# An adaLN linear-attention and MLP block on one core: w_mod's products on TensorE directly, and the first two k projections side by side

## The chip, the core and the metric

The kernel runs on 1 core of a Trainium2 chip. The core has TensorE (matrix products, PE in the profile; PEld is its loading of weights), VectorE (DVE), ScalarE (ACT), GpSimd (POOL) and SyncE (SP), which issues DMAs. The metric is device time in microseconds (us). Times are the median of several executions; a profile is one execution recorded by the hardware profiler.

## What is computed

The inputs are x (2048 tokens, D = 576 features), wqkv (576 x 1728), wo (576 x 576), w1 (576 x 4608), w2 (4608 x 576), a condition c (1 x 576) and w_mod (576 x 3456), all in float32. Cut to what matters, the reference is:

```
mod = silu(c) @ w_mod                     # six vectors of 576: sa, ca, ga, sb, cb, gb
h = layernorm(x) * (1 + ca) + sa
q, k, v = split(h @ wqkv)                 # 32 heads of 18 features
kv = sum over tokens of phi(k) x v;  z = sum over tokens of phi(k)
x = x + ga * ((phi(q) kv / (phi(q) z)) @ wo)
h = layernorm(x) * (1 + cb) + sb
x = x + gb * (silu(h @ w1) @ w2)
```

with phi(t) = t + 1 for positive t and exp(t) otherwise, plus 1e-6. sa and ca are needed before the first projection. They are the first third of w_mod ("piece 0", 1152 columns: 576 for the shift, 576 for the scale).

## The kernel before, in words

Tokens are worked in 16 tiles of 128, in four blocks of four tiles. The 576 features are cut in five chunks along the contraction, four of 128 and a tail of 64. Operands of the large products are split in a high and a low part (float32r), so a projection of one tile is a row of 14 passes over chunk and part (`x_passes`, L208), each pass with two products of about half the output columns: 28 products a tile.

**The opening (L255 to L375)** is written in a fixed order on all engines (`manual_schedule`). SP issues the loads: c, the four x tiles of block 0, piece 0 of w_mod in five chunks, then wqkv in three groups (k, v, q) of five chunks; the tail's rows are loaded twice, into partitions 0 to 63 and 64 to 127. The silu of c stands as a column per chunk in `sc`. The product c @ w_mod is made in two ways:

- the first chunk of w_mod goes to TensorE directly (`mod_mm`, L272): stationary is a 128-column piece of w_mod, moving a 128 x 128 tile that holds the chunk's c in every column (`scb`);
- the other four chunks are multiplied by their c and summed on VectorE (L334 to L339) into `sums`, which TensorE then turns into columns with a tile of ones (`mod_cols`, L347).

The result is one column of shift and one of scale per chunk (`cols["a"]`, L352). Meanwhile the four x tiles are normalised (`LayerNorm`, L151) and transposed on TensorE (L331) into PSUM banks, one of 512 columns per chunk: the four tiles side by side. Each chunk is then modulated over all 512 columns (L185 on ScalarE, L187 on VectorE) and split in high and low part (`split_h`, L189: a copy on ScalarE L191, a subtraction on VectorE L109) into `hT`. Chunks go in the order 0, 2, 4, 1, 3. The weights' high parts are copies on ScalarE (`w_hi`, L281), their low parts subtractions on VectorE or GpSimd (`w_lo`, L284).

**The loop over the 16 tiles (L478)** does per tile the k projection (`k_proj`, L423) with phi, the v projection (`v_proj`, L431), the product of keys and values of the tile before (`kv_mm`, L446), and on some tiles a q projection (`q_proj`, L441). PSUM has two large buffers for projections (`ps2`, name psK), one bank for transposes (`psT`) and the sums of keys and values (kvp). The block after is normalised and transposed (`turn`, L470) inside the loop. The other two thirds of w_mod are summed on VectorE at tiles 5 and 8 (`mod_piece`, L378) from three raw buffers. In the loop a planner orders each engine's instructions by its own estimate of time; `behind(...)` holds work back until given instructions have been issued.

**After the loop** (from L528) come the last q projections, the attention output, and the MLP in two-block units. Some lists of order are written out by hand (`ORDERS`, L64); they begin after the loop.

## Time and profile before

| | us |
|---|---|
| median of 3 runs | 1156.73 (1156.49 to 1158.33) |
| the profiled execution, whole | 1160.13 |
| its span, first to last instruction | 1158.4 |
| TensorE busy in the span | 1135.1 |
| VectorE busy | 977.3 |
| GpSimd busy | 659.7 |
| ScalarE busy | 527.8 |

A line of a group view reads: source line, engine, operation, output and inputs, shapes, count | busy us in all, mean ns of one | idle time of the engine before it, and what ended that. A line of the timeline reads: start, length, engine, line, operation, count, and in brackets idle time before it and who ended it. Neighbouring instructions of one kind are one line there. A line of waits reads: who waited for whom, us in total, times, longest. Matmuls are pipelined: the length of a single one includes the way through the array, so the cost of many is read from a group's length.

### The profile page before, as it was taken

The numbers are of one execution on the slowest core, as the hardware profiler recorded it, in microseconds if no ns is written. First come the engines' busy times: TensorE is split into PE (matmuls) and PEld (weight loads), VectorE is DVE, ScalarE is ACT, GpSimd is POOL, SyncE is SP. The second block draws the span as 40 slices with busy tenths as digits, with TensorE's granted clock in tenths as the row PEclk, the third lists the DMA queues.
The fourth block names the chain that finished last, engine by engine and source line by source line (L and its number), as shares of the span: only waits on it lengthen the run. The fifth ranks groups of instructions, "written<-read, shape, count | busy, mean of one in ns | idle before, by whom it ended". The sixth has DMA issues, their size and how long they took to land.

```text
span 1158.4 us, 19498 instructions
## 1 busy us (share of the span) xinstructions
PE 1135.1 (98%) x7173; PEld 1049.7 (91%) x7173; DVE 977.3 (84%) x1540; ACT 527.8 (46%) x1074; POOL 659.7 (57%) x749
## 2 busy tenths in 40 slices
PE   4999999999999999999999999999999999999998
PEld 4999999999998889999999999999999999999998
DVE  6747664478797999999999999999999999999996
ACT  4443343336656445444444444454444444444541
POOL 4300000254635495776777677767757766776686
PEclk9999999999999999999999999999999999999999
DMA  9213300123157978869769769778687697697684
GB/s 284 105 42 93 113 6 1 32 69 130 41 230 268 377 260 305 320 251 350 274 253 349 273 252 364 265 278 334 260 329 299 251 352 272 253 354 274 251 311 154
DMA packets 57213, 268.61 MB, mean 232 GB/s; under 512 B 5466, under 2 KB 19294, under 8 KB 34078
## 3 DMA queue, kind: packets, MB, share of 16 engines
q1 hardware_dynamic: 57118, 267.36, 62.8%
q8 instruction: 57, 0.93, 0.3%
q14 instruction: 38, 0.31, 0.1%
HBM read 250.56 MB, written 16.78 MB: 231 GB/s over the span
## 4 chain that ended last, share of the span: by engine, by line
PE 94%; DMA 2%; DVE 1%; ACT 1%; issue 0%; SPq 0%; ACTq 0%; DVEq 0%
PE up L1142 33%; PE down L1215 32%; PE psK L212 13%; PE big L212 7%; PE small L705 2%; PE big L716 2%; PE kvp L452 1%; DMA acc<-in_A_wqkv_dram 1%; PE psK L599 1%; PE big L631 1%; PE small L200 1%; DVE hT L109 1%; PE psT L200 1%; DMA hT<-in_w_mod_dram 1%; PE up L1245 1%; PE down L1245 1%
## 5 line engine op out<-in xcount | busy, mean ns | idle before, releaser
L1223 DVE TENSOR_TENSOR acc<-down,acc 128x576 f32<-128x576 f32 x330 | 246.0, 753 | 13.3 <-PE down L1215 3.3
L1142 PE MATMUL up<-hT,w 128*128 128x512 f32 x916 | 240.3, 391 | 0.0
L1142 PEld LDWEIGHTS up<-hT,w 128*128 128x128 f32 x916 | 164.5, 188 | 25.8
L1177 POOL TENSOR_TENSOR s<-f,f 128x256 f32<-128x256 f32 x66 | 51.7, 784 | 163.8 <-ACT f L1158 163.8
L1215 PE MATMUL down<-w,hb 128*128 128x288 f32 x792 | 120.7, 294 | 0.0
L1215 PE MATMUL down<-w,hc 128*128 128x288 f32 x792 | 120.7, 294 | 0.0
L1215 PEld LDWEIGHTS down<-w,hb 128*128 128x128 f32 x792 | 113.5, 188 | 6.1 <-DVE U L1223 0.5
L1215 PEld LDWEIGHTS down<-w,hc 128*128 128x128 f32 x792 | 113.6, 188 | 5.6
L212 PE MATMUL psK<-w,hT 128*128 128x288 f32 (+1 forms) x704 | 112.7, 300 | 3.1 <-DVE hT L109 2.1
L1223 DVE TENSOR_TENSOR U<-down,U 128x576 f32<-128x576 f32 x132 | 99.5, 753 | 17.4 <-PE down L1215 15.1
L109 DVE TENSOR_TENSOR w<-v,w 128x288 fp32r<-128x288 f32 (+1 forms) x170 | 111.9, 668 | 0.4 <-ACT w L885 0.4
L212 PEld LDWEIGHTS psK<-w,hT 128*128 128x128 f32 x704 | 100.8, 191 | 4.4 <-DVE hT L109 3.1
L1142 PE MATMUL up<-room,w 128*128 128x512 f32 x348 | 93.2, 396 | 0.9 <-DVE f L1163 0.9
L1196 POOL TENSOR_TENSOR hc<-s,hc 128x512 fp32r<-128x512 f32 x66 | 89.7, 1359 | 0.0
L1158 ACT ACTIVATE f<-f 128x512 f32<-128x512 f32 x102 | 64.4, 631 | 47.8 <-DVE f L1163 25.4
L1161 DVE TENSOR_TENSOR f<-up,p 128x512 f32<-128x512 f32 x102 | 69.7, 683 | 15.4 <-PE up L1142 9.7
L1142 PEld LDWEIGHTS up<-room,w 128*128 128x128 f32 x348 | 62.4, 188 | 12.2 <-DVE f L1163 1.4
L885 ACT CAST w<-v 128x288 fp32r<-128x288 f32 x85 | 36.6, 434 | 77.0 <-PE down L1215 54.3
L1181 POOL TENSOR_TENSOR f<-f,s 128x256 f32<-128x256 f32 x66 | 50.9, 772 | 34.4 <-DVE hb L1196 28.7
L1215 PE MATMUL down<-w,hd 128*128 128x288 f32 x396 | 63.2, 295 | 0.0
L1215 PE MATMUL down<-w,he 128*128 128x288 f32 x396 | 63.1, 295 | 0.0
L1215 PE MATMUL down<-w,ha 128*128 128x288 f32 x396 | 63.0, 294 | 0.0
(281 smaller groups left out, 2468.8 us busy)
## 6 DMA issues: line engine op xcount, KB each, us to landing
hT<-hd SPq DMA_DIRECT2D x66, 1280.0 KB, 6.0
hT<-hd SPq DMA_DIRECT2D x45, 1024.0 KB, 5.1
room<-hd SPq DMA_DIRECT2D x35, 1280.0 KB, 5.6
room<-hd SPq DMA_DIRECT2D x20, 1024.0 KB, 5.6
v<-in_B_w_dram SPq DMA_DIRECT2D x17, 576.0 KB
v<-in_B_w_dram SPq DMA_DIRECT2D x17, 512.0 KB, 7.8
hd<-S SPq DMA_DIRECT2D x6, 1024.0 KB, 4.2
xt<-in_A_x_dram SPq DMA_DIRECT2D x16, 288.0 KB, 4.2
```

What stands on the lines that cost most here:

```text
L109: return V.tensor_sub(lo, full, f32(hi))
L200: T.transpose(ps[:, i * P : (i + 1) * P], xt[i][:, cidx * P : (cidx + 1) * P], ident)
L212: T.matmul(ps, xpart(a), wpart(b), start=n == 0, stop=n == len(XW) - 1)
L885: A.copy(self.w2[n][:, 0], src)
L1142: T.matmul(ps, left, right, start=first and m == 0, stop=m == len(seq) - 1, skip_group_check=True)
L1158: A.activation(self.f[i, k], self.f[i, k], AF.Silu)
L1161: V.tensor_add(f, self.bank[bank[1]], self.p1)
L1177: G.tensor_add(self.s[:, 0:1], half(i, 0, 1), half(i, 1, 1))
L1181: G.tensor_sub(half(i, 1, 0), half(i, 1, 0), self.s[:, 1:2])
L1196: eng.tensor_sub(t[:, :, 1, :], src, f32(t[:, :, 0, :]))
L1215: T.matmul(ps[:, p, :HALF], self.a[i, n][:, u, p * P : (p + 1) * P], self.w.w2[n][:, v], start=n in (1, 5, 7, 6) and j == 0, stop=j == 2, ...
L1223: V.tensor_add(dst, ps[:, :, :HALF], dst)
```

## The change

- **Loads.** c is loaded from ScalarE's queue instead of SP's. c's tail is written twice into its row, so that the tail's c stands in partitions 0 to 63 and again in 64 to 127. w_mod's tail of piece 0 is loaded from ScalarE's queue in two loads: the rows' shift half into partitions 0 to 63, their scale half into 64 to 127. Chunks are loaded in order 0 to 4.
- **w_mod.** Chunks 0 and 1 (`mod_direct`) and the tail go to TensorE directly. The moving operand is a single column of c; for the tail it is a tile of two columns, `sel`, so that one product gives shift and scale. VectorE sums chunks 2 and 3 only, first the columns of feature chunks 0 and 1 (HEAD = 2), then the rest (`add_mod`, `col_mod`); TensorE turns these sums with one column of ones.
- **Block 0 in two halves.** Tiles 0 and 1 are transposed, modulated and split first (256 columns a chunk). As each chunk is ready, `k_part` runs its first two passes for both tiles; the passes with the weights' low parts and those of the tail follow, tile by tile. So both k projections fill both large PSUM buffers at the same time. Their phi (`k_phi`) and the split of the result (`k_split`) are written out in the opening too, as are the splits of v's weights.
- **The second half.** Tiles 2 and 3 are transposed, modulated and split (`turn_half`) beside the v projections of tiles 0 and 1. Scratch for the halves is the three raw buffers.
- **The loop.** TensorE's instructions are kept in the order of the program text; k of tiles 0 and 1 is left out. In `x_passes` the chunks go 0 to 4.

The core of the diff:

```diff
-    CHUNKS = (0, 2, 4, 1, 3)
+    CHUNKS, START = (0, 2, 4, 1, 3), range(KC + 1)
     XW = []
-    for k in CHUNKS:
+    for k in START:
...
-    nc.sync.dma_start(crow[0:KC, :], c[0, 0 : KC * P].rearrange("(j p) -> j p", p=P))
-    nc.sync.dma_start(crow[KC : KC + 1, 0:64], c[0:1, KC * P : D])
-    xts = [load_x(0, i) for i in range(4)]
+    nc.scalar.dma_start(crow[0:KC, :], c[0, 0 : KC * P].rearrange("(j p) -> j p", p=P))
+    nc.scalar.dma_start(crow[KC : KC + 1, :].rearrange("p (h r) -> p h r", h=2),
+                        c[0:1, KC * P : D].unsqueeze(1).to_broadcast([1, 2, 64]))
+    xts = x0s = [load_x(0, i) for i in range(4)]
...
+    load_mod(mods[0], 0, 0)
+    for a in range(2):
+        nc.scalar.dma_start(tmod[a * 64 : a * 64 + 64, 0:D], w_mod[KC * P : D, a * D : (a + 1) * D])
+    for k in range(1, KC):
         load_mod(mods[k], 0, k)
...
+    def mod_mm(m, k, rhs, a=None, first=False, last=False):
+        c = 2 * (k - HEAD if k >= HEAD else k)
+        dst = mod_ps_a[k >= HEAD][:, c : c + 2] if a is None else mod_ps_a[k >= HEAD][:, c + a : c + a + 1]
+        T.matmul(dst, m[:, k * P : (k + 1) * P], rhs, start=first, stop=last, skip_group_check=True)
+
+    def mod_direct(m, rhs, first=False):
+        A.copy(m[:, :, D:DX], m[:, :, KC * P : D])
+        for k in START:
+            for a in range(2):
+                mod_mm(m[:, a], k, rhs, a, first and k in (0, HEAD) and a == 0)
+
+    def add_mod(k0, k1):
+        o = sums[:, :, k0 * P : min(k1 * P, D)]
+        V.scalar_tensor_tensor(o, mods[3][:, :, k0 * P : min(k1 * P, D)], sc[:, 3:4], o, op0=ALU.mult, op1=ALU.add)
...
+    def turn_half(chunks):
+        t = psT()
+        pT = {k: t[:, n * 256 : n * 256 + 256] for n, k in enumerate(chunks)}
+        turn_tiles(pT, (2, 3), chunks)
+        for k in chunks:
+            modulate_split(*half_args(1, k, pT))
+
+    def k_part(tiles, passes, first=False, last=False):
+        for n, (a, b) in enumerate(passes):
+            for i in tiles:
+                for h in range(2):
+                    T.matmul(kps[i][:, h, :HALF], hT[0][:, a, i * P : i * P + P], wk_(b)[:, h * HALF : (h + 1) * HALF],
+                             start=first and n == 0, stop=last and n == len(passes) - 1)
...
+        mod_direct(mods[0], sc[:, 0:1], True)
+        A.copy(tmod[:, D:DX], tmod[:, KC * P : D])
+        for k in START:
+            mod_mm(tmod, k, sel)
+        ln.normalise(0, xts[0], xts[0], V)
+        ln.normalise(1, xts[1], xts[1], A)
...
+        turn_tiles(pT, (0, 1), range(KC))
+        mod_direct(mods[1], sc[:, 1:2])
+        for i in (2, 3):
             ln.normalise(i, xts[i], xts[i], A)
...
+        add_mod(0, HEAD)
+        col_mod(0, HEAD)
+        modulate(*args[0], V)
+        w_hi(wk_, 0, acc[0])
+        split_h(*args[0])
+        modulate(*args[1], A)
+        add_mod(HEAD, KC + 1)
+        first_k(0)
+        col_mod(HEAD, KC + 1)
...
+        for k in START:
+            w_lo(wk_, k, acc[k], G if k < 3 else V)
+        for i in range(2):
+            k_part([i], [(k, KC + k) for k in START[:KC]] + [(2 * KC + 1, 2 * KC), (2 * KC, 2 * KC)], last=True)
...
+        a0 = k_phi(kps[0])
...
+        first = *k_split(0, a0), pool
+        after = *k_split(1, k_phi(kps[1])), pool
...
-    for t in range(NT):
+    with tc.manual_schedule(engines={mybir.EngineType.PE}):
+        for t in range(NT):
...
+            if t > 1:
+                k_proj(t)
...
+            if t == 0:
+                with behind(first):
+                    turn_half((0, 1))
             before, after = after, v_proj(t)
+            if t == 0:
+                with behind(first):
+                    for k in START:
+                        split_w(wqp_, k, acc[10 + k], G)
+                    turn_half((2, 3))
+            if t == 1:
+                turn_half((4,))
```

More of the change, by code (lines that the diff above doesn't have):

```diff
@@ L270 @@
     vx = [pa.tile([P, NHC, 2, P], F32R, name=f"vx{i}") for i in range(2)]
-    def mod_mm(ps, m, kp, k, rhs, first, last):
-        for a in range(2):
-            T.matmul(ps[:, a * P : (a + 1) * P], m[:kp, a, k * P : (k + 1) * P], rhs,
-                     start=first and a == 0, stop=last, skip_group_check=True)
     def mod_ps(k):
@@ L295, with k_phi, k_split @@
+    def k_phi(ps):
+        a = pa.tile([P, D], F32, name="a")
+        phi(ps, a, pa)
+        return a
+    def k_split(t, a):
+        return A.copy(pk[t % 2][:, 0, :D], a), sub_hi(pk[t % 2][:, 1, :D], a, pk[t % 2][:, 0, :D])
     wk_, wv_ = cut(wkv, 0, D), cut(wkv, D, D)
-    ND = 1
-    scb = pa.tile([P, D], F32, name="e", bufs=2)[:, : ND * P].rearrange("p (k q) -> p k q", k=ND)
-    sums = mods[ND]
+    sums = mods[2]
+    sel = pa.tile([P, 2], F32, name="sel")
+    h32 = [pa.tile([P, 2, D], F32, name="raw", bufs=3).rearrange("p a d -> p (a d)") for _ in range(3)]
@@ new lines, in col_mod, with turn_tiles @@
+    def col_mod(k0, k1):
+        for k in range(k0, k1):
+            for a in range(2):
+                mod_mm(sums[:, a], k, ones[:, 0:1], a, last=True)
+        V.tensor_add(cols["a"][:, k0:k1, :], mod_ps_a[k0 >= HEAD].rearrange("p (k a) -> p k a", a=2),
+                     plus1.unsqueeze(1).to_broadcast([P, k1 - k0, 2]))
+    def turn_tiles(pT, tiles, chunks):
+        for i in tiles:
+            for k in chunks:
+                T.transpose(pT[k][:, i % 2 * P : i % 2 * P + P], x0s[i][:, k * P : (k + 1) * P], ident)
```

225 lines of the change are left out of this document (101 added, 124 removed).

## The prediction

> **What bounds the kernel now.** I read the page first (shares, then the chain that ended last), then TensorE's stretches, its waits, and the order of its instructions in the first 60 us.
>
> ```profile
> span 1158.4 us, 19498 instructions
> ...
> PE 1135.1 (98%) x7173; PEld 1049.7 (91%) x7173; DVE 977.3 (84%) x1540; ACT 527.8 (46%) x1074; POOL 659.7 (57%) x749
> ...
> PE 94%; DMA 2%; DVE 1%; ACT 1%; issue 0%; SPq 0%; ACTq 0%; DVEq 0%
> ```
>
> TensorE carries 94% of the last chain. The rest is the opening, so the next view cuts TensorE's time there (columns: stretch, length, busy time and instructions, granted clock, DMA share, GB/s).
>
> ```profile
> core 0: us, PE busy (x), PEclk, DMA share, GB/s
> 9.80:13.00 3.20, 3.17 (x15) 1.00 1.04 392
> 13.00:16.40 3.40, 2.97 (x27) 1.00 1.06 245
> 16.40:19.80 3.40, 1.16 (x8) 1.00 1.04 274
> 19.80:23.20 3.40, 3.27 (x14) 0.50 1.06 293
> 23.20:26.60 3.40, 2.05 (x12) 1.00 1.06 338
> 26.60:30.00 3.40, 1.68 (x9) 1.00 1.05 299
> 30.00:33.40 3.40, 3.40 (x15) 0.50 1.06 399
> 33.40:60.00 26.60, 26.60 (x204) 1.00 0.13 50
> 60.00:240.00 180.00, 177.46 (x1307) 1.00 0.16 48
> 240.00:1158.40 918.40, 913.11 (x5572) 1.00 0.73 271
> ```
>
> From 30 us on there is next to no idle time: 2.5 us up to 240, 5.3 us after. So a gain is work that TensorE has finished earlier when it becomes continuously busy, and it lasts to the end. There are holes before 30 us, and two stretches at half clock, each after a thinly used one.
>
> ```profile
> 9.80 3.80 PEld L275 LDWEIGHTS kvp<-e,hT 128*128 128x128 f32 x20 [5.63 <-issue]
> 9.83 3.96 PE L275 MATMUL kvp<-e,hT 128*128 128x128 f32 x20 [5.57 <-DMA hT<-in_w_mod_dram]
> ...
> 15.36 1.42 DVE L339 SCALAR_TENSOR_TENSOR hT<-hT,sc 128x1152 f32<-128x1152 f32 x1 [1.11 <-DMA hT<-in_w_mod_dram]
> ...
> 18.28 1.40 ACT L282 CAST w<-acc 128x576 fp32r<-128x576 f32 x2 [5.28 <-DMA acc<-in_A_wqkv_dram]
> ...
> 22.64 0.75 PE L212 MATMUL psK<-w,hT 128*128 128x288 f32 x2
> ...
> 32.83 2.84 PE L212 MATMUL psK<-w,hT 128*128 128x256 f32 x18
> ...
> 54.00 0.50 PE L212 MATMUL psK<-w,hT 128*128 128x288 f32 x2
> ```
>
> The rows give the opening's dates: the first w_mod chunk lands at 9.8, the last full one at 15.4, k's first weights at 18.3. Tile 0's k projection begins at 22.64, v of tile 0 at 32.8, and k of tile 2 at 54.0. Between 22.6 and 32.8 only one k projection is done, because:
>
> ```profile
> PE psK L212 <- DVE hT L109: 2.1, 4, 0.8
> PE kvp L275 <- DVE hT L339: 2.0, 1, 2.0
> PE psK L212 <- ACT hT L191: 0.9, 1, 0.9
> ```
>
> TensorE waits for VectorE's sum of w_mod (L339) and then, chunk by chunk, for the split of the block (L191, L109).
>
> **The yardstick.** I compare the date at which k of tile 2 begins. By then the kernel before has also done the key-value product of tile 1 (10 instructions) and four transposes, which the new order puts later: 10 x 0.133 (3.73/28, below) and 4 x 0.14 (2.2/16) = 1.9 us. So the date to beat is 54.0 - 1.9 = 52.1.
>
> **The change, priced from these rows.**
>
> ```profile
> 1.26 0.36 SPq L256 DMA_DIRECT2D crow<-in_c_dram  x1
> ...
> 49.95 3.73 PE psK L212 x28
> ...
> 108.03 1.28 PE L396 MATMUL psK<-ones,tmod 128*128 128x128 f32 x10
> ...
> L333 PE MATMUL psK<-ident,xt 128*128 128x128 f32 x16 | 2.2, 272 | 0.0
> ...
> L187 DVE TENSOR_SCALAR a<-psT,col_a 128x512 f32<-128x512 f32 x1 | 0.8, 801 | 0.0
> ...
> L191 ACT CAST hT<-h 128x512 fp32r<-128x512 f32 x2 | 1.2, 620 | 0.0
> ...
> L109 DVE TENSOR_TENSOR hT<-e,hT 128x512 fp32r<-128x512 f32 x2 | 2.6, 1290 | 0.0
> ...
> L414 DVE TENSOR_SCALAR a<-psK 128x576 f32<-128x576 f32 x3 | 2.3, 756 | 2.1 <-ACT e L409 2.1
> ...
> L409 ACT ACTIVATE e<-psK 128x576 f32<-128x576 f32 x5 | 3.2, 646 | 5.3 <-PE psK L212 5.3
> ```
>
> *Loads.* c moves from SP to ScalarE's queue, so the x tiles are issued two issues earlier; w_mod's tail (288 KB) travels beside them. The bytes are the same, and the DMA share is full anyway. I take the first w_mod chunk at 10.0 instead of 9.8, the last full one unchanged at 15.4. The four issues on ScalarE stand ahead of work that isn't needed before 10 us; without that cover they would cost some 1.4 us (4 x 0.36, SP's issue of c).
>
> *w_mod on TensorE.* Two full chunks and the tail are multiplied directly: 10 + 10 + 5 products, each recorded as two instructions, with one or two columns moving instead of 128. VectorE loses two of its four sums (1.4 us for a full chunk) ahead of the first column. The trace has no one-column product. Bounds: zero, and the price with 128 columns, 0.128 us an instruction (1.28/10) or, from a standing start, 0.198 (3.96/20). I take 0.09 and 0.17, near the top, because the weight loads alone fill 3.80 of the 3.96 us and none is saved. Then: 10.0 + 20 x 0.17 = 13.4; the tail, 10 x 0.09, 14.3; eight transposes at 0.14 (2.2/16), 15.4; second chunk, 1.8, 17.2. VectorE's sum for the first two columns (512 of 1152 elements, 0.63 us after 15.4) is ready at 16.0, so TensorE is late, not VectorE. Four more products, 0.7, and the small addition, taken at 0.2: the first columns stand at X = 18.1. With a free one-column product VectorE sets X at 16.2; with 128-column prices X is 20.2.
>
> *First half-block.* Only 256 columns are modulated and split, so modulation (0.80) and split copy (0.62) become about 0.45 and 0.36; the subtraction (1.29 on the mean, 0.65 by size) is taken at 0.5, as GpSimd's subtractions run beside fewer of them. First k products at X + 0.9. VectorE then sums the other three columns (0.79 + 0.2), TensorE turns them (12 x 0.09 = 1.1), and chunk 1 begins at X + 3.9. From there ScalarE is the pace: cast of weights 0.67, split 0.36, part of the modulation, some 1.1 us a chunk, against 8 x 0.133 = 1.07 on TensorE. Chunk 3 ends at X + 7.5. The last two low parts of the weights follow on VectorE (taken at 0.75 each, like L414's pass over 576 columns) and the remaining 24 products end at X + 11.2 = 29.3: both k projections done, where before one was done at 32.8.
>
> *v of tile 0* needs a bank of tile 0's k: exponent and maximum (0.65 + 0.76) end at 29.3 behind four weight splits on VectorE. It begins at 29.4. Then 28 products for each of v0, v1, q0, q1 (4 x 3.73), one key-value product (1.33) and ten transposes of the second half, no longer in an idle stretch (1.4): 29.4 + 17.65 = 47.05. Against 52.1 that is 5.1 us.
>
> *What is late next.* The second half's transposes share one bank, so chunks 2 and 3 wait for ScalarE's modulation of 0 and 1 (up to 2 us; 1.0 taken). And q's weights:
>
> ```profile
> 39.47 2.85 POOL L287 TENSOR_TENSOR wq<-acc,wq 128x576 fp32r<-128x576 f32 x2 [10.20 <-ACT wq L282]
> ...
> 43.91 3.81 POOL L287 TENSOR_TENSOR wq<-acc,wq 128x576 fp32r<-128x576 f32 x2
> ...
> 18.10:52.20 34.10, 30.25 (x198) 28.87 (x199) 27.07 (x51) 20.16 (x38) 16.55 (x11) 0.90 0.57 187
> ```
>
> GpSimd's five subtractions for wq span 8.3 us (39.47 to 47.7). With q0 starting at 39.3 and needing the last at 42.5, they must begin by 34; ScalarE's casts now may start ahead of v0's eviction. And VectorE's 27.1 us of work (third busy figure) must fit into 28.9 (18.1 to 47.0) instead of 34.1. Together 0.7 us taken, none to 3 the bounds. The gain left is 5.1 - 1.7 = 3.4 us.
>
> *Moved at no cost.*
>
> ```profile
> xt<-in_A_x_dram SPq DMA_DIRECT2D x16, 288.0 KB, 4.2
> ...
> L164 DVE BATCH_NORM_STATS2 st<-xt 128x6 f32<-128x288 f32 x16 | 6.2, 442 | 3.7 <-DMA xt<-in_A_x_dram 3.7
> ...
> L170 POOL TENSOR_TENSOR rstd<-ve,neghalf 128x4 f32<-128x4 f32 x2 | 2.1, 1030 | 5.0 <-DVE ve L169 5.0
> ...
> L177 ACT ACTIVATE xt<-xt,nm,rstd 128x576 f32<-128x576 f32 x4 | 3.5, 863 | 0.1
> ```
>
> The two x tiles of the second half keep their buffers until the last transposes after v1, about 38.4, so block 1's last two tiles land near 42.6 (4.2 from issue). Statistics 4 x 0.39, the power 1.03, normalising 2 x 0.87 on ScalarE and some 1.5 of small steps: 48.4. Their first transposes come after k of tile 2, 47.05 + 3.73 = 50.8: 2.4 us of cover, then 1:1. The raw w_mod loads wait for the half-block's scratch, from 30 to some 41, for a use after 90. TensorE's order written out for tiles 2 to 15 replaces a planned one with 2.5 us of idle time (60 to 240): zero taken, between -2.5 and +2.5. Chunk order 0 to 4 changes no count.
>
> [...] The rows at 0.50 are 3.4 us long and follow stretches with 1.16 and 1.68 us of work; 2.05 us was enough. [...] Whether one-column products count no run here shows; by a reading in which they don't, the first rival comes out. [...]
>
> **The rivals.**
>
> *Slower: half clock through the opening.* [...] For: half-clock rows follow stretches with up to 1.68 us of products. Against: 9.8 to 13.0 is dense and is followed by a full-clock stretch. Price at 0.2 an instruction: 10.0 + 4.0 + 2.0 + 1.6 + 4.0 + 1.6, X = 23.4. Chunk 0 ends at 26.2, the other columns 2.4 later, transposes 0.4, chunks 1 to 3 one window at 0.23 and the rest full, 33.7; 24 more, 36.9; + 17.65 + 1 of stall = 55.55: 3.4 us slower, 1160.1. It breaks even near 0.15 us an instruction in that stretch.
>
> *No change: the head start is given back.* q0 waits for GpSimd's wq (1.8 us if the casts begin only after v0's eviction), the transposes for ScalarE (2.0), VectorE's overload delays block 1 (about 1.3): the 5.1 us are gone, 1156.7. For: VectorE is busy 27.1 of 34.1 us already, and wq was just in time. Against: TensorE never stopped from 33.4 to 60.
>
> *More gain.* Free one-column products (X = 16.2) and no stall: 5.1 + 1.9 = 7.0, 1149.7.
>
> **How the numbers follow.** The profiled execution took 1160.13 us, 3.4 above the median of the three runs (1156.73); the sum is a difference of dates, so it is taken off the median: 1156.73 - 3.4 = 1153.3. What a measurement here tells from no change is 0.2%, 2.3 us. Chances: the forecast 0.52, more gain 0.03, the head start given back 0.24, half clock 0.21. Hence faster 0.55, same 0.24, slower 0.21. The likeliest case's own range is 1150.8 to 1154.4; the range given, 1150.8 to 1159.2, takes in most of the other two.
>
> **What would show it.** Right: one-column instructions at 0.06 to 0.12 us; first k product at 18 to 20; both k projections done near 29; k of tile 2 beginning at 47 to 50; no 0.50 row between 20 and 40. Wrong: 0.50 rows from 16 to 27, TensorE waiting for wq (L287), for hT in the second half, or for xt at block 1. The forecast falls if X is past 21, or if idle time between 60 and 240 grows by more than 2 us.

## The result, and the profile after

| us | before | after |
|---|---|---|
| median (runs) | 1157.53 (4, 1156.49 to 1161.54) | 1169.68 (4, 1168.43 to 1169.99) |
| the profiled execution, whole | 1160.13 | 1169.40 |
| its span | 1158.4 | 1167.7 |
| k of tile 2 begins | 54.0 (52.1 on the same work) | 61.95 |

The changed kernel is slower: ratio 1.0096, 95% interval 1.0070 to 1.0122. The forecast was 1153.3 us, faster. By dates: 61.95 - 52.1 = 9.85 us are lost before k of tile 2, and 0.55 us come back after it (1167.7 - 61.95 against 1158.4 - 52.1), which makes the 9.3 us between the two spans. The medians differ by 12.15 us. Of these, 2.6 us are the profiled execution of before, which lay above its median; no date shows where those went.

The page of the changed kernel: span, shares, and the chain that ended last.

```profile
span 1167.7 us, 19567 instructions
...
PE 1144.4 (98%) x7203; PEld 1058.8 (91%) x7203; DVE 977.4 (84%) x1539; ACT 531.2 (45%) x1088; POOL 660.1 (57%) x749
...
PE 94%; DVE 2%; DMA 2%; ACT 1%; issue 0%; SPq 0%; DVEq 0%; ACTq 0%
```

TensorE still sets the end and is busy 9.3 us longer for 30 instructions more. So it is slower per instruction somewhere. The stretches of the opening (busy time and count of PE, PEld, DVE, ACT, POOL; granted clock; DMA share; GB/s) show where:

```profile
13.00:16.40 3.40, 3.40 (x17) 3.40 (x18) 1.57 (x2) 2.91 (x5) 0.26 (x1) 1.00 1.05 391
16.40:19.80 3.40, 3.40 (x18) 3.40 (x18) 0.00 (x0) 0.00 (x0) 1.15 (x1) 1.00 1.05 281
19.80:23.20 3.40, 3.40 (x18) 3.40 (x17) 0.00 (x0) 0.00 (x0) 0.00 (x0) 1.00 1.07 312
23.20:26.60 3.40, 2.13 (x10) 2.04 (x11) 1.70 (x4) 1.43 (x4) 0.00 (x0) 1.00 1.05 345
26.60:29.40 2.80, 2.80 (x15) 2.79 (x14) 1.54 (x2) 0.31 (x1) 1.42 (x1) 1.00 0.24 54
29.40:33.40 4.00, 3.63 (x28) 3.31 (x28) 2.27 (x5) 2.43 (x5) 1.16 (x1) 1.00 0.35 120
33.40:53.30 19.90, 16.25 (x109) 14.34 (x108) 19.08 (x24) 14.36 (x31) 12.45 (x8) 1.00 0.22 68
53.30:56.70 3.40, 3.40 (x16) 3.40 (x15) 3.40 (x14) 0.22 (x1) 0.00 (x0) 0.50 0.75 214
...
60.00:240.00 180.00, 178.16 (x1323) 174.74 (x1323) 103.65 (x193) 70.14 (x135) 12.60 (x15) 1.00 0.15 46
```

Three things are to be seen. From 13 to 23 us TensorE is busy without a gap, but with 17 or 18 instructions in 3.4 us (those cut by the edges are counted too), some 0.2 us each; VectorE and ScalarE stand still from 16.4 to 23.2 and wait for it. From 33.4 to 53.3 it is the other way round: VectorE is full (19.08 of 19.9), and TensorE is idle for 3.65 us of it. From 53.3 to 56.7 the clock is at half. The clock column needs care: it reads 1.00 where the trace holds no clock record. The first record of this trace, full clock, begins at 29.4; before it the pace of the instructions has to tell, and e1 below, which has records there, shows that it is the pace of half clock. Here are TensorE's rows of the opening:

```profile
10.25 4.40 PE L329 MATMUL kvp<-sc,hT 128*128 128x1 f32 x20 [5.11 <-DMA hT<-in_w_mod_dram]
14.51 2.27 PE L329 MATMUL kvp<-sel,tmod 128*128 128x2 f32 x10
16.64 0.67 PE L354 MATMUL psT<-ident,xt 128*128 128x128 f32 x2
...
18.38 4.26 PE L329 MATMUL kvp<-sc,hT 128*128 128x1 f32 x20
22.51 1.84 PE L329 MATMUL kvp<-ones,hT 128*128 128x1 f32 x8
25.63 1.33 PE L371 MATMUL psK<-w,hT 128*128 128x288 f32 x4 [1.27 <-ACT hT L191]
...
28.57 1.78 PE L329 MATMUL kvp<-ones,hT 128*128 128x1 f32 x12
...
30.80 2.74 PE L371 MATMUL psK<-w,hT 128*128 128x288 f32 x16
...
39.15 0.54 PE L212 MATMUL psK<-w,hT 128*128 128x256 f32 x2
...
52.97 9.15 PE L212 MATMUL psK<-wq,hT 128*128 128x288 f32 x56
61.95 0.43 PE L212 MATMUL psK<-w,hT 128*128 128x288 f32 x2
```

Twenty one-column instructions take 4.3 us, 0.21 each. The first columns stand at 24.5 (forecast 18.1), the first k product at 25.63, and both k projections are done at 39.2 (forecast 29.3), when v of tile 0 begins; the 56 products of q begin at 52.97, k of tile 2 at 61.95. VectorE's rows, from the small copy in the opening to the last part of v of tile 0 (timeline of the changed kernel):

```profile
26.86 1.31 DVE L342 COPY hT<-hT 128x128 f32<-128x128 f32 x1
...
41.73 1.99 DVE L109 TENSOR_TENSOR pk<-a,pk 128x576 fp32r<-128x576 f32 x1
...
45.54 3.22 DVE L109 TENSOR_TENSOR hT<-raw,hT 128x256 fp32r<-128x256 f32 x2
48.68 0.41 DVE L109 TENSOR_TENSOR vx<-psK,vx 128x252 fp32r<-128x252 f32 x1
49.01 1.65 DVE L109 TENSOR_TENSOR pk<-a,pk 128x576 fp32r<-128x576 f32 x1
...
52.47 0.22 DVE L109 TENSOR_TENSOR vx<-psK,vx 128x72 fp32r<-128x72 f32 x1
```

And GpSimd's, from the same timeline:

```profile
26.68 1.42 POOL L287 TENSOR_TENSOR w<-acc,w 128x576 fp32r<-128x576 f32 x1 [9.12 <-ACT w L282]
...
43.18 6.86 POOL L287 TENSOR_TENSOR wq<-acc,wq 128x576 fp32r<-128x576 f32 x4
50.11 1.81 POOL L289 TENSOR_TENSOR wq<-acc,wq 64x576 fp32r<-64x576 f32 x1
```

The last low part of v of tile 0 is written from 52.47 to 52.7, and the product of keys and values waits for it. TensorE's waits:

```profile
PE kvp L517 <- DVE vx L109: 2.1, 2, 1.1
...
PE psK L371 <- ACT hT L191: 1.3, 1, 1.3
```

So the loss has three places. My forecast for k of tile 2 was 48.75; it came 13.2 us later: 6.4 up to the first columns, 3.5 from there to the end of both k projections (14.7 us instead of 11.2), and 3.4 from there to k of tile 2 (22.8 us from the start of v of tile 0, instead of 19.35 from a forecast start at 29.4). The experiments take them one by one.

### The profile page after: what moved, and what is told of

It reads as the page before. It is cut to its first block, busy times and chain, and to the rows that moved or that the text cites. A ratio compares the mean times of both kernels' runs of the same rounds, so it can differ in the third digit from the quotient of the medians.

```text
span 1167.7 us, 19567 instructions
## 1 busy us (share of the span) xinstructions
PE 1144.4 (98%) x7203; PEld 1058.8 (91%) x7203; DVE 977.4 (84%) x1539; ACT 531.2 (45%) x1088; POOL 660.1 (57%) x749
## 4 chain that ended last, share of the span: by engine, by line
PE 94%; DVE 2%; DMA 2%; ACT 1%; issue 0%; SPq 0%; DVEq 0%; ACTq 0%
PE up L1211 33%; PE down L1284 31%; PE psK L212 12%; PE big L212 7%; PE small L774 2%; PE big L785 2%; PE kvp L517 1%; PE kvp L329 1%; PE psK L668 1%; PE big L700 1%; DMA room<-hd 1%; DVE hT L109 1%; PE small L200 1%; DMA hT<-in_w_mod_dram 1%; PE up L1314 1%; PE down L1314 1%
## 5 line engine op out<-in xcount | busy, mean ns | idle before, releaser
L212 PE MATMUL psK<-w,hT 128*128 128x288 f32 (+2 forms) x660 | 108.0, 298 | 0.8 <-DVE w L287 0.6
L212 PEld LDWEIGHTS psK<-w,hT 128*128 128x128 f32 x660 | 95.0, 189 | 1.5 <-DVE w L287 0.8
L1230 DVE TENSOR_TENSOR f<-up,p 128x512 f32<-128x512 f32 x102 | 69.7, 683 | 14.7 <-PE up L1211 10.1
L954 ACT CAST w<-v 128x288 fp32r<-128x288 f32 x85 | 36.5, 434 | 77.0 <-PE down L1284 52.1
```

What stands on the lines that cost most here:

```text
L212: T.matmul(ps, xpart(a), wpart(b), start=n == 0, stop=n == len(XW) - 1)
L954: A.copy(self.w2[n][:, 0], src)
L1230: V.tensor_add(f, self.bank[bank[1]], self.p1)
```

## The experiments

Executions of one kernel scatter: the kernel before ran from 1155.56 to 1161.98 us in eleven. So single times tell only differences of several us. I read the dates in the traces, which all lie in the first 65 us; the time is given beside them. A date carries some luck too: with the same opening the clock came up at 29.4 in the changed kernel, at 34.7 in e10 and e15 and at 36.5 in e11, and the stage from the first k product to both k done took 13.5 us in the one and 14.3 in the other three. A half-clock stretch in q's 56 products, which some runs have and others don't, is worth another 1.3 to 1.5 us. So a difference of a date below some 1.5 us behind the opening can be this luck. "kv waits" is the time that the first product of keys and values waits for v.

| run | first k product | both k done | kv waits | k of tile 2 | span |
|---|---|---|---|---|---|
| before | 22.64 | | | 54.0 (52.1) | 1158.4 |
| after | 25.63 | 39.15 | 2.1 | 61.95 | 1167.7 |
| e1 dense products ahead | 24.10 | 38.37 | 2.1 | 59.66 | 1164.9 |
| e2 128 columns | 23.18 | 35.22 | 2.0 | 58.02 | 1163.2 |
| e3, e20 chunk 1 and tail on VectorE | 19.27, 20.62 | 33.98, 34.24 | 2.2, 2.1 | 55.24, 56.99 | 1159.9, 1162.3 |
| e4 planned order | 25.67 | 40.60 | 3.0 | 64.92 | 1171.3 |
| e5 wq's low parts on VectorE | 25.78 | 39.25 | 2.2 | 62.09 | 1166.7 |
| e8a e3 + e2 + dense products | 19.26 | 32.76 | 2.2 | 54.03 | 1161.5 |
| e8b the same, planned order | 21.82 | 35.35 | 3.0 | 59.78 | 1166.5 |
| e10 no low parts of wq | 25.63 | 39.92 | 0.5 | 59.05 | 1165.6 |
| e11 c and tail on SP | 27.54 | 41.82 | 2.1 | 63.08 | 1168.4 |
| e13 wq and half block behind v | 25.71 | 38.92 | 0 | 63.26 | 1170.0 |
| e14 e3 + e13 | 19.39 | 34.64 | 0 | 57.70 | 1165.5 |
| e15 only wq behind v | 26.04 | 40.31 | 0 | 63.91 | 1171.3 |
| e16 no k by chunks | 29.97 | 40.18 | 2.0 | 61.77 | 1166.6 |
| e17, e18 e15 on e8a, on e3 | 21.12, 19.06 | 34.64, 33.76 | 0, 0 | 55.73, 54.82 | 1162.3, 1160.5 |
| e19 e8a + e10 | 18.85 | 33.50 | 0.5 | 52.57 | 1164.5 |

**Is it the clock?** e1 puts dense products of ones (128 columns, into a bank that is free) into the idle time ahead of the opening's sums and changes nothing else.

```diff
+        wps = ps2()
+        for n in range(8):
+            T.matmul(wps[:, 0, :P], ones, ones, start=True, stop=True)
         psc = psT()[:, : KC + 1]
         T.transpose(psc, crow, ident[: KC + 1, : KC + 1])
         A.activation(sc, psc, AF.Silu)
+        for n in range(12):
+            T.matmul(wps[:, 0, :P], ones, ones, start=True, stop=True)
```

> The changed kernel with 20 products of a tile of ones (128 columns, float32) put on TensorE while it waits, 8 before c and 12 after c has been turned; nothing else differs. Theory 1, the clock: the one-column products do not count as work, so the changed kernel's opening ran at half clock until k's own products, to 29.7 us; with dense work ahead the clock is full by about 8 us and falls back some 3 to 7 us after the last dense product. Then the first chunk's 20 instructions take 2.2 us instead of 4.4, the first columns stand at 18 to 20 us instead of 24.5, and the time falls by 5 us or more, to about 1163. Theory 2, the weight loads: a one-column product costs its load of weights, about 0.2 us, at any clock; then 4.4 us stay 4.4 and the time stays at 1168 to 1170.

Measured: 1166.60 us. The clock is full from 9.15 us. TensorE's rows in e1's timeline:

```profile
10.56 2.57 PE L329 MATMUL kvp<-sc,hT 128*128 128x1 f32 x20 [0.19 <-DMA hT<-in_w_mod_dram]
12.99 2.27 PE L329 MATMUL kvp<-sel,tmod 128*128 128x2 f32 x10
...
16.86 4.26 PE L329 MATMUL kvp<-sc,hT 128*128 128x1 f32 x20
```

Its stretches (columns as above):

```profile
9.15:12.57 3.42, 3.23 (x30) 3.06 (x28) 2.00 (x7) 1.37 (x4) 1.03 (x1) 1.00 1.03 395
12.57:15.98 3.41, 3.41 (x18) 3.41 (x18) 1.57 (x2) 3.25 (x7) 0.00 (x0) 0.50 1.06 395
15.98:33.05 17.07, 15.55 (x72) 15.36 (x71) 5.92 (x10) 4.55 (x10) 4.24 (x3) 0.50 0.80 240
```

This is the sharpest reading of all. The clock falls at 12.57, inside the first row of twenty: the eighteen instructions that begin before it take 2.00 us, 0.11 each, and from there on each takes 0.21. The 128-column products of ones just ahead of them, at the same full clock, also take 0.11. And the full clock is lost after one stretch of 3.42 us in which TensorE was busy for 3.23 us: 1.2 us with the last products of ones, 2.0 us with one-column products. It comes back only at 33.05, when k's own products have run. Here the one-column products took time, but they didn't hold the clock. As the clock fell so soon, the first columns came at 23.0, not at the 18 to 20 expected, and the time fell by 3.1 us, not by 5.

e2 gives the products for the columns of feature chunks 0 and 1 128 moving columns, those for the others 32 (the tail's, which make shift and scale at once, 256 and 64). ScalarE writes the wider operands; the number of products stays.

```diff
+    NW = 128, 32
...
+        n = NW[k >= HEAD]
...
+        rhs = rhs[k >= HEAD].rearrange("p a n -> p (a n)") if a is None else rhs[:, :n]
         T.matmul(dst, m[:, k * P : (k + 1) * P], rhs, start=first, stop=last, skip_group_check=True)
...
-        mod_direct(mods[0], sc[:, 0:1], True)
+        mod_direct(mods[0], scw[0], True)
```

> The changed kernel with wide moving operands in the products of w_mod: 128 columns for the feature chunks 0 and 1, 32 for the others, instead of one or two. The same number of products and weight loads. Theory 1, the clock: the wide products count, the clock goes full some 3 to 7 us after the first of them, as in the kernel before (13.0 us); the first columns stand at 19 to 21 us instead of 24.5, and the time falls by 4 us or more although each product moves more data. Theory 2, the weight loads: wider products can only cost more; the first columns stand at 24.5 or later and the time does not fall.

Measured: 1164.89 us. TensorE's rows in e2's timeline:

```profile
10.11 4.45 PE L335 MATMUL kvp<-e,hT 128*128 128x128 f32 x20 [5.63 <-DMA hT<-in_w_mod_dram]
14.37 3.23 PE L335 MATMUL kvp<-e,tmod 128*128 128x256 f32 x10
...
18.62 2.32 PE L335 MATMUL kvp<-e,hT 128*128 128x128 f32 x20
20.77 1.14 PE L335 MATMUL kvp<-ones,hT 128*128 128x128 f32 x8
```

The groups of twenty are eight instructions with 128 columns and twelve with 32. They take 4.45 us at half clock and 2.32 at full clock, as they do with one column (4.40; e1, 2.57 with the last two at half clock). Only the tail's ten, four of them with 256 columns, cost more (3.0 us, against 2.13). The first columns come at 22.1, later than the 19 to 21 expected, as the clock came up only at 18.1, behind the tail. So the cut of the moving operand to one column saved nothing. It cost the clock: in e2 it is full from 18.1 to 48.8 (in the changed kernel from 29.4), and k of tile 2 comes 3.9 us earlier than in the changed kernel, though each product moves more. Which of the three widths (32, 128 or 256) brought the clock up, this run can't say.

**w_mod's direct products, undone in part.** e3 gives chunk 1 and the tail back to VectorE's sum (the tail is then loaded once, into 64 partitions); chunk 0 stays direct, with one column.

```diff
+        V.scalar_tensor_tensor(o[:64], tmod[:64, :, k0 * P : min(k1 * P, D)], sc[:64, 4:5], o[:64], op0=ALU.mult, op1=ALU.add)
...
-        A.copy(tmod[:, D:DX], tmod[:, KC * P : D])
-        for k in START:
-            mod_mm(tmod, k, sel)
...
-        mod_direct(mods[1], sc[:, 1:2])
...
-        V.tensor_scalar(sums[:, :, 0:D], sums[:, :, 0:D], sc[:, 2:3], None, op0=ALU.mult)
+        V.tensor_scalar(sums[:, :, 0:D], sums[:, :, 0:D], sc[:, 1:2], None, op0=ALU.mult)
+        V.scalar_tensor_tensor(sums[:, :, 0:D], mods[2][:, :, 0:D], sc[:, 2:3], sums[:, :, 0:D], op0=ALU.mult, op1=ALU.add)
```

> One part undone: w_mod's chunk 1 and its tail go back to VectorE's sum; only chunk 0 is multiplied on TensorE directly, still with one column. 30 recorded instructions of TensorE fewer ahead of the first columns. Both theories expect the first columns near 19 us instead of 24.5 (30 x 0.22 = 6.6 us less on TensorE, VectorE about 17). Theory 1 adds that the clock is still half until k's own products have run for a stretch, so that the chunk stage (14.7 us from first columns to both k projections done) gets no shorter; theory 2 alone would let it fall towards the 11.2 us predicted. Time 1163 to 1165 by both.

Measured: 1161.63 us, k of tile 2 at 55.24. The same kernel was timed over more executions (e20):

> The changed kernel with chunk 1 and the tail of w_mod back on VectorE's sum, as before, in three rounds beside the kernel before: theory, 1.5 to 4 us slower than it (1161.6 against 1159.6 in the first run), with k of tile 2 at 55.0 to 55.5. Rival (the first run was a chance of the clock's windows): level, within 1 us.

Measured: 1163.29 us median of 8 against 1159.37 of before (11), run beside it, ratio 1.0047 (1.0026 to 1.0068). So roughly half of the loss, 0.5 of 0.96% by two separate comparisons, belongs to chunk 1 and the tail on TensorE. The first k product comes 5.0 to 6.4 us earlier without them. k of tile 2 missed the expectation by 1.5 us: 56.99 against 55.24 in the first run, 1.3 us of it from one half-clock stretch in q's 56 products (8.96 against 7.62 us). The same kernel meets it or not.

**Is it the order?** e4 lets the planner order TensorE in the loop, as before.

```diff
-    with tc.manual_schedule(engines={mybir.EngineType.PE}):
+    with ExitStack():
         for t in range(NT):
```

> One part undone: in the loop over the tiles TensorE's order is the planner's again instead of the text's. Theory 4, the order: TensorE stood 2.1 us before the first key-value product although q of tiles 0 and 1 could have run, and the thin stretch brought 3.4 us of half clock. With the planner's order q comes first: k of tile 2 begins at 58 to 60 us instead of 61.95. Rival: q's weights are not split before 50 to 52 us either (GpSimd), so TensorE waits for them instead; 61.5 or later. Both theories leave the opening alone: first columns at 24.5, both k projections done near 39.

Measured: 1172.99 us, k of tile 2 at 64.92. From v of tile 0 to there it takes 24.3 us, against 22.8 by the text's order, which is so the better one; it isn't the cause.

**What makes kv wait for v?** e5 gives wq's five low parts to VectorE.

```diff
-                        split_w(wqp_, k, acc[10 + k], G)
+                        split_w(wqp_, k, acc[10 + k], V)
```

> The changed kernel with the five low parts of q's weights subtracted on VectorE instead of GpSimd. Theory 3, contention: from 40 to 52 us VectorE's subtractions took 1.6 to 2.0 us beside GpSimd's where they take 0.41 to 0.76 alone, so v of tile 0 was moved out of its bank 9 us late, TensorE stood 2.1 us before the key-value product and then ran 3.4 us at half clock. Without GpSimd's subtractions the five extra ones cost VectorE 3.8 us but the others become short: k of tile 2 begins 2 to 4 us earlier than 61.95. Rival: VectorE is simply full in that stretch and five more instructions make it later; k of tile 2 begins at 62 or later.

Measured: 1168.37 us, kv waits 2.2, k of tile 2 at 62.09: no change, so the rival's forecast held. VectorE took on 3.5 us of work and was not later. e10 leaves that work out altogether (wq's low parts are zeros, which GpSimd writes at the start).

```diff
-                        split_w(wqp_, k, acc[10 + k], G)
+                        A.copy(wqp_(k) if k < KC else wqp_(2 * KC)[:64], acc[10 + k] if k < KC else acc[10 + k][:64])
```

> The changed kernel, but the low parts of wq are never computed: GpSimd writes zeros there at the start, and ScalarE still copies the high parts, so the projections of q are coarser by that part. It takes 8.7 us of subtractions from GpSimd between 43 and 52 us and gives them to nobody. Theory (VectorE's subtractions are long only beside GpSimd's: 1.61 and 1.8 to 2.0 us where the same forms take 0.41 and 0.75 us with GpSimd idle): the rows of hT<-raw and pk in 40 to 52 us fall to 0.4 to 0.8 us, the first kv products no longer wait for v's low part of tile 0 (2.1 us in the changed kernel; 0.5 us or less here), TensorE keeps its full clock there, and k of tile 2 starts at 58.3 to 59.8 us instead of 61.95; span 1164 to 1165.8. Rival (VectorE has more work than time there, as the run with wq's subtractions on VectorE suggested): the wait stays above 1.5 us and k of tile 2 at 61 us or later; span 1166.5 or more.

Measured: 1167.28 us, kv waits 0.5, k of tile 2 at 59.05, the clock full throughout from 34.7 and q's 56 products in 7.63 us (9.15 in the changed kernel). From v of tile 0 to k of tile 2 it takes 19.1 us (22.8 in the changed kernel, 19.35 forecast). VectorE's groups from 43 to 52.9 us show why. In the changed kernel:

```profile
L109 DVE TENSOR_TENSOR hT<-raw,hT 128x256 fp32r<-128x256 f32 x4 | 4.5, 1170 | 0.0
L109 DVE TENSOR_TENSOR pk<-a,pk 128x576 fp32r<-128x576 f32 x2 | 3.6, 1818 | 0.0
```

In e5, the same view:

```profile
L287 DVE TENSOR_TENSOR wq<-acc,wq 128x576 fp32r<-128x576 f32 x4 | 2.8, 753 | 0.0
...
L109 DVE TENSOR_TENSOR hT<-raw,hT 128x256 fp32r<-128x256 f32 x5 | 1.9, 419 | 0.0
```

And in e10:

```profile
L109 DVE TENSOR_TENSOR pk<-a,pk 128x576 fp32r<-128x576 f32 x2 | 2.7, 1368 | 0.0
...
L109 DVE TENSOR_TENSOR hT<-raw,hT 128x256 fp32r<-128x256 f32 x4 | 1.5, 417 | 0.0
```

VectorE's subtraction of two 256-column operands takes 0.42 us alone and 1.17 on the mean beside GpSimd's subtractions. GpSimd needs 6.86 us for the four low parts that VectorE does in 2.8. So in this stretch the two engines don't work side by side: work given to GpSimd is paid for by VectorE, 3.0 us on these four subtractions (4 x 0.75). A plain copy of 128 columns on VectorE (L342) shows it too: in the changed kernel it began at 26.86, 0.18 us after a GpSimd subtraction, and ended at 28.17, with it (28.10), 1.31 us in all; in e3 (at 22.45), with GpSimd idle from 21.75 to 27.09, it took 0.23. Why the two hold each other up no run here shows.

Can the order help? e13 moves the splits of wq and two chunks of the half block behind v's eviction, e15 only the splits of wq, and e14 is e13 on e3.

```diff
-                with behind(first):
+                with behind(after):                # e13, e14: both; e15: only the loop over split_w
                     for k in START:
                         split_w(wqp_, k, acc[10 + k], G)
                     turn_half((2, 3))
```

> The changed kernel with the splits of wq and the transposes and splits of two chunks of the half block behind v's eviction of tile 0 (they stand behind k's split of tile 0 in the changed kernel). Theory (kv waits since v's low part of tile 0 stands in VectorE's line behind other work): v's eviction comes first, the first kv products wait 0.5 us or less for it, and k of tile 2 starts at 59.5 to 61.0 us; span 1165.3 to 1167. Rival (whatever is put behind is late next): q's first product or the half block of hT waits in its place, k of tile 2 at 61.5 or later, span 1167.3 or more.

> The same order of v's eviction in the kernel whose chunk 1 and tail of w_mod go back to VectorE's sum (1161.6 us, k of tile 2 at 55.24, kv waits 2.2 us). Theory: the wait goes, k of tile 2 at 53.0 to 54.3, span 1157.5 to 1159.0, level with the kernel before. Rival: 55 us or later, span 1159.5 or more.

> The changed kernel with only the splits of wq behind v's eviction of tile 0; the half block's transposes stay where they are. Theory (GpSimd's subtractions for wq, side by side with VectorE's from 43 to 52 us, make the wait of kv; the order of the half block was what hurt when both were moved): v's low part of tile 0 is out before GpSimd begins, kv waits 0.8 us or less, k of tile 2 at 59.0 to 60.5 us; span 1164.5 to 1166.5. Rival (q's products then wait for wq's low parts): q's 56 products take 1.5 us longer or more, k of tile 2 at 61.0 or later.

Measured: 1171.71, 1167.24 and 1173.03 us. kv waits no more in any of them, and k of tile 2 is later in all three than in what they start from. From v of tile 0 on it takes 24.3, 23.1 and 23.6 us (22.8 in the changed kernel; 21.3 in e3, without the half-clock stretch that q has in the others); of e15's 2.0 us, 1.2 were lost before that. In e13 and e14 the last transposes of the half block wait 2.8 us for ScalarE's modulation, in e15 q waits for wq's low parts, piece by piece (1.65 us). TensorE's rows in e15's timeline:

```profile
52.70 1.06 PE L212 MATMUL psK<-wq,hT 128*128 128x288 f32 x6 [0.32 <-POOL wq L287]
...
56.95 0.79 PE L212 MATMUL psK<-wq,hT 128*128 128x288 f32 x4 [0.70 <-POOL wq L289]
58.58 5.49 PE L212 MATMUL psK<-wq,hT 128*128 128x288 f32 x28 [0.84 <-DVE mv L165]
```

The wait went, as my theory (kv is late because of its place in the line) had it, but the loss stayed, and the rival held each time: something must be last, since, as I read e5 and e10, the sum of VectorE's and GpSimd's work doesn't fit.

**What are the products chunk by chunk worth?** e16 issues both tiles' k products tile by tile after the last chunk's split.

```diff
         def first_k(k):
-            k_part(range(2), [(k, k), (KC + k, k)], k == 0)
+            pass
...
-            k_part([i], [(k, KC + k) for k in START[:KC]] + [(2 * KC + 1, 2 * KC), (2 * KC, 2 * KC)], last=True)
+            k_part([i], [(b, k) for k in START[:KC] for b in (k, KC + k)] + [(k, KC + k) for k in START[:KC]] + [(2 * KC + 1, 2 * KC), (2 * KC, 2 * KC)], True, True)
```

> The changed kernel without the k products chunk by chunk: both tiles' 56 products are issued one tile after the other, when the last chunk is split; all else the same. Theory (the chunk stage is bound by TensorE at half clock and by the splits, and the early products hide under it): 32 products no longer lie beside the splits, both k projections end at 42.5 to 45 instead of 39.2, k of tile 2 at 64.5 to 67; span 1170 to 1173.5. Rival (the feed alone sets the end, the early products are worth nothing): both k end at 40.5 or earlier, k of tile 2 at 63 or earlier.

Measured: 1168.32 us, both k done at 40.18, k of tile 2 at 61.77. The rival held: 1.0 us at the end of the k stage, and none at k of tile 2 (0.2 earlier than in the changed kernel). TensorE started 4.3 us later and took 10.2 us for the 56 products, the first 5.4 us at half clock. In the changed kernel only 8 of the 56 products run before 30 us; that is all the head start there is.

**The second queue.** e11 puts c and the tail of w_mod back on SP's queue.

```diff
-    nc.scalar.dma_start(crow[0:KC, :], c[0, 0 : KC * P].rearrange("(j p) -> j p", p=P))
+    nc.sync.dma_start(crow[0:KC, :], c[0, 0 : KC * P].rearrange("(j p) -> j p", p=P))
...
-        nc.scalar.dma_start(tmod[a * 64 : a * 64 + 64, 0:D], w_mod[KC * P : D, a * D : (a + 1) * D])
+        nc.sync.dma_start(tmod[a * 64 : a * 64 + 64, 0:D], w_mod[KC * P : D, a * D : (a + 1) * D])
```

> The changed kernel with c and the tail of w_mod back on SP's queue, in the same order; nothing else. Theory: the second queue is worth a few tenths of a us at the start (x and the chunks of w_mod come that much later behind c and the tail), and k of tile 2 starts at 61.7 to 63.0 us; span 1167.5 to 1169. Rival (the 64-row transfers of the second queue hold up the chunks of w_mod, and with them the opening): k of tile 2 at 61.0 or earlier, span below 1167.

Measured: 1170.08 us. The first product on w_mod begins at 12.16 instead of 10.25, the first k product 1.9 us later, k of tile 2 1.1 us later. By these dates this part of the change is a gain of some 2 us in the opening, more than I expected; in one run each the two times, 0.4 us apart, can't tell it from nothing.

**With the terms mended.** e8a adds dense products and 128 or 32 columns to e3 (e1's 20, and the 14 below); e8b is e8a in the planner's order; e9 gives the kernel before dense products alone (8 ahead of c, 12 behind it, 8 ahead of the sum, 8 behind a split).

```diff
+        def dense(n):
+            for _ in range(n):
+                T.matmul(kps[1][:, 0, :P], ones, ones, start=True, stop=True)
...
         add_mod(0, HEAD)
+        dense(10)
         col_mod(0, HEAD)
+        dense(4)
```

> What the runs so far say is put together: w_mod's chunk 1 and tail on VectorE, moving operands of 128 and 32 columns, and dense products of a tile of ones where TensorE would stand idle (20 before the first w_mod chunk, 10 before and 4 after the first columns). Theory 1, the clock, with the price of the weight loads: the clock is full from about 9.5 us to the end of the opening; first columns at 16.5 to 18, first k product at 18 to 19, both k projections done at 29 to 31 (10.3 to 11.9 us after the first k product, as at full clock before, not 14.7). k of tile 2 begins at 50 to 52.5, the time is 1156 to 1160, level with the kernel before. If the chunk stage still takes 14 us or more at full clock, it is VectorE and ScalarE that set it and not the clock.

> The same with the planner's order in the loop over the tiles. If the order of the key-value product costs what theory 4 says, k of tile 2 begins 1 to 2.5 us before that of the same kernel with the text's order; if q's weights are the limit, at the same time.

> The kernel before, with dense products of ones where TensorE stands idle: 20 before the first w_mod chunk, 8 after the transposes, 8 beside the first k projection. Theory 1: its two half-clock stretches (19.8 to 23.2 and 30.0 to 33.4) go, each worth 1 to 1.7 us; k of tile 2 begins at 51.0 to 52.8 instead of 54.0 and the time falls by 1 to 3 us. If the fillers stand in the way of the k projection, 54 or later.

Measured: 1163.17, 1168.22 and 1160.98 us; k of tile 2 at 54.03, 59.78 and (e9) 53.67. e9 gained 0.3 us at that date, not 1.2 or more, but it doesn't tell what the clock is worth to the kernel before: its clock is at half from 11.5 to 15.0 and from 28.6 to 32.0, two stretches of 3.4 us as in the kernel before, only at other places. e8a is 1.9 us behind the 52.1 of before, later than the 50 to 52.5 expected; it too has a half-clock stretch, from 24.1 to 27.5. e17 and e18 add e15's order to e8a and e3, and e19 adds e10 to e8a, so that the opening and the overload are mended together, with dense products for the clock:

> Chunk 1 and the tail of w_mod back on VectorE, 128 moving columns, dense products of ones before the opening's sums (1163.2 us, k of tile 2 at 54.03), and wq's splits behind v's eviction. Theory: k of tile 2 at 51.5 to 53.0, span 1157.5 to 1160. Rival: q waits for wq's low parts, 54 or later.

> Chunk 1 and the tail of w_mod back on VectorE (1161.6 us, k of tile 2 at 55.24), and wq's splits behind v's eviction, without the products of ones. Theory: k of tile 2 at 52.5 to 54.0, span 1157.3 to 1159.0, level with the kernel before. Rival: q waits for wq's low parts, 55 or later.

> Chunk 1 and the tail of w_mod on VectorE, 128 moving columns and dense products of ones before the sums (1163.2 us, k of tile 2 at 54.03, kv waits 2.2 us), and in addition wq's low parts left out (GpSimd writes zeros there at the start), which coarsens the projections of q. With that the clock, the opening's late date and the overload of VectorE and GpSimd are all mended at once, as far as runs can. Theory (these three are the whole loss up to k of tile 2): k of tile 2 at 51.0 to 52.3, level with the 52.1 of the kernel before on the same work, still without the gain of 3.4 us forecast (48.75), since the chunk stage takes 13.5 us from the first k product at any clock; span 1157.5 to 1159.5. Rival (the chunk stage also gets shorter without GpSimd): 50 or earlier, span below 1157.

Measured: 1163.96, 1162.26 and 1166.19 us; k of tile 2 at 55.73, 54.82 and 52.57. From v of tile 0 to that date e17 and e18 take 21.1 us, 0.2 less than e8a and e3: q waits 1.7 us for wq where kv waited 2.2 for v. What e17 loses to e8a it loses before, in the opening (first k product at 21.12 against 19.26), with the clock at half from 11.0 to 17.9. e19 comes within 0.5 us of before (52.57 against 52.1), 0.3 us later than the theory's range, with the clock at half from 22.8 to 29.6. But its span, 1164.5, is 5 us above the range: after k of tile 2 it takes 1111.9 us (before 1106.3). 3.4 us of this are two half-clock stretches of 3.4 us from 145.6 us on, around waits of 1.8 and 0.8 us for VectorE. Why these came isn't settled. No version ran faster than the kernel before.

## Why the prediction was wrong

**The yardstick and the loads** were right: the first w_mod chunk at 10.25 (forecast 10.0), VectorE's sum for the first columns ready in time (TensorE late, not VectorE), 9.85 us at k of tile 2 against 9.3 in the span, idle time from 60 to 240 us 1.8 (before 2.5) against "zero taken".

**The step that failed is "w_mod on TensorE": 0.17 us an instruction from a standing start and 0.09 in flow.** The 58 one- and two-column instructions up to the first columns were to take 6.8 us and took 12.4, 0.214 each; with the transposes (0.6) and the start (0.25) that is the 6.4 us by which X came late (24.5 instead of 18.1). The size was right for a full clock: by e1's 0.11 they would take 6.5. The error lies in which clock they get. The row of before that I priced from, "3.96/20 from a standing start", already held both prices: in its trace the first fourteen instructions follow each other at 0.21 us and the last six at 0.11, with the step at 12.95, where its first clock record begins. I had the half clock as the first rival, with X = 23.4, a break-even near 0.15 us an instruction and a chance of 0.21; the measured X lies 1.1 us beyond it. The evidence I held against it was "9.8 to 13.0 is dense and is followed by a full-clock stretch". But that stretch moved 128 columns, and I carried its clock over to one column. Which products hold the clock I had left open; the trace of before, put beside e1, says more. Its stretch from 12.95 to 16.36, 0.7 us of 128-column products and then 2.2 us of transposes, kept the full clock; the next one, with 1.16 us of 128-column products alone, lost it, and so did e1's, with 1.2 us of them and 2.0 us of one-column products. So here transposes did help to hold the clock, and the one-column products didn't.

**"Both k projections done at X + 11.2"** took X + 14.7. Chunk 1 began at X + 6.3 (30.80) instead of X + 3.9: TensorE, still at half clock, came from chunk 0 and four transposes to the twelve products at 28.57 and took 1.8 us for them, not 1.1. The small copy "taken at 0.2" took 1.31 behind GpSimd, but it was done at 28.2, before TensorE came to it. From chunk 1 on the rest took 8.35 us instead of 7.3. In e2, at full clock, the stage from the first k product is 12.0 us instead of 13.5. In e8b and e17, at full clock too, it is 13.5 all the same: there chunk 1 and the tail are VectorE's, and TensorE waits 1.4 and 1.5 us for that sum. So clock and feed share this term, and I can't divide it further.

**"What is late next", 1.7 us taken**, was 5.1 (1.7 and the 3.4 lost beyond it). The direction was right: VectorE's overload. Of the 3.4, 1.6 us are kv's wait for v (2.1 against 0.5 in e10), 1.5 the half-clock stretch in q's products (9.15 against 7.63 us), which in e10 is gone, with the wait or by the grid's place (below); the other 0.3 us are spread. I had bounded VectorE's overload by its busy time, 27.1 us in a stretch of 28.9. That count took the durations of before as fixed, and took GpSimd's 16.6 us as work beside it. They are not beside it.

**The rival "half clock through the opening"** gave k of tile 2 at 55.55 and 1160.1 us; measured are 61.95 and 1169.7. Of the 6.4 us between the dates, 1.1 came up to X, 1.15 in the stage behind it and 4.15 from v of tile 0 on, where the other rival's overload came on top: I had priced the two as alternatives, and both fell due together. The other 3.2 us of the time lie in none of these dates. I had taken dates from an execution of before 3.4 us above its median and added their difference to the median, and no run shows where that execution lost its 3.4 us. The range given, up to 1159.2, left out this rival's own price, and the time went 10 us past it. The later X also moved VectorE's work together: it idled from 16.4 to 23.2 and was full from 33.4 to 56.7.

## What to carry to other kernels

Before moving sums from VectorE to TensorE as products with one moving column, price them at what an instruction cost here with 1 as with 128 moving columns (0.11 us each at full clock, 0.21 at half) and ask what keeps the clock up: with 128 columns it came up by 13 us in the kernel before, with one column not before 29.4 in the changed kernel. When work is spread over VectorE and GpSimd, don't lay the times that each takes alone side by side (here VectorE's 0.42 us became 1.17), and test it by leaving the work out, as e10 does: where e13 to e15 moved it, the wait moved with it. When two rivals rest on different engines, price the case in which both come true.

## What the runs showed of the hardware

- One stretch of 3.4 us with 2.0 us of one-column products ended a full clock (e1, at 12.57), though TensorE was busy for 3.23 us of it; a stretch with 2.2 us of transposes and 0.7 us of 128-column products kept it (before, 12.95 to 16.36). And 15 us of one-column products and transposes, with a gap of 1.3 us, never started it (changed kernel, 10.25 to 25.6; it came at 29.4, after the first 8 k products).
- An instruction with 128 stationary columns costs the same with 1 and with 128 moving columns: 0.11 us at full clock in e1 (eighteen in 2.00 us from 10.56 on, and the products of ones ahead of them), 0.21 us at half clock (one column: 4.26/20 in the changed kernel; 128 columns: the first fourteen from 9.83 on in before).
- The half-clock stretches end and begin on a grid of 3.41 us that differs from run to run (the clock changes at 12.95, 19.77, 23.19, 30.01 and 33.43 in the kernel before, at 29.40, 53.29 and 56.71 in the changed one): the same kernel had none in q's products (7.62 us) in one execution and one (8.96 us) in another. In e2, with 128 and 32 columns from 10.11 on, the clock came up at 18.1, behind the tail's 256 columns, while in the kernel before twenty instructions with 128 columns from 9.83 on were enough for a full clock by 13; which share of wide products it takes isn't settled.
- Five low parts of 576 columns on GpSimd take 8.7 us, and VectorE's two-operand subtractions of 256 columns beside them 1.17 us instead of 0.42; the same five on VectorE take 3.5 us, and those subtractions 0.42 (e5).
